# Ordering a weight load behind a one-column activation, and moving two small matmul events to the edges of a projection stage

## The chip, the cores and the metric

The kernel runs on one core of a Trainium2 chip. The metric is device time of one execution in microseconds (us), lower is better. Everything below is a matter of less than 1% of the time, so each comparison uses several runs, and the kernel before was timed again, on the same chip, beside every group of experiments (the four groups of experiments ran on four different chips). All runs reported here count as of the fast state, at a granted TensorE clock of 0.999 to 1.0, but for two runs of e9 at 0.996.

The engines are called TensorE (PE in the profile; PEld is its weight load), VectorE (DVE), ScalarE (ACT), GpSimd (POOL) and SyncE (SP). ACTq and SPq are the queues on which ScalarE and SyncE issue DMA transfers. PSUM is where the program puts TensorE's outputs; it does so in eight buffers of up to 512 columns, called banks here, four in the pool `ps_pj` and four in `ps_1`. A transfer has landed when the last of its completion marks has arrived, of which the packed traces show 16 for each transfer of the start; landing times here are read from these marks. The pitch is the time from one matmul's start to the next one's. Stages are called by the tile that TensorE writes in them: pk_ps (first projection), g_ps, kv_ps (KV), p_ps (projections of the V stage), q_ps (the quads).

## The reference, cut to what matters

Two attention blocks on the same x (2048 x 1024) are mixed by a sigmoid gate. Block A is linear attention, block B a dilated sliding window of 8 keys; 32 heads of 32.

```python
def phi(t): return where(t > 0, t + 1, exp(t)) + 1e-6
# A: pq, pk = phi(q), phi(k)
kv  = einsum("bhsd,bhse->bhde", pk, v)
num = einsum("bhqd,bhde->bhqe", pq, kv)
den = einsum("bhqd,bhd->bhq", pq, z)[..., None] + 1e-6   # z: pk summed over s
a   = (num / den) @ wo_A
# B: softmax over 8 earlier keys at distance 2, then @ wo_B      [cut]
out = g * a + (1 - g) * b
```

The kernel folds KV into A's output weight: the product of KV and `wo_A`, called W2 here, replaces `WoA` in place.

## The kernel before

The parts that the change touches, in the order in which TensorE meets them. At the start, the first projection (`pk`) needs `xT`, which comes by DMA transposes on SyncE's queue, and `WkA`, of which the first two quarters (k rows 0 and 1; column halves 0 and 1) come on ScalarE's queue. `project` runs the first k slice of half 0 for token tiles 0 to 3, of 128 tokens each (8 matmuls), then of half 1.

```python
load_wk(nc.scalar, 0, 0)                       # first quarter, 256 KB
first_act = consts.tile([P, 1], BF16, name="first_act")
nc.scalar.activation(out=first_act[:], in_=ones[:, 0:1], func=ACT.Exp)
load_wk(nc.scalar, 0, 1)                       # second quarter
load_xT(0, 0, 2)                               # transposes, SyncE
load_xT(0, 2, 4)
for k in range(1, 4):
    load_wk(nc.sync, k, 0); load_xT(k, 0, 4); load_wk(nc.sync, k, 1)
# ... [cut]
warm_up(37)                                    # 37 small matmuls
```

Later, KV is accumulated, then the V projection of B runs, with the four W2 events strewn into its first 64 matmuls, and with A's query projection (`qa`) from the fifth token tile on:

```python
for g in range(2):
    kvp = ps_1.tile([P, 4, 64], F32, name="kv_ps", tag="p1")
    # ... 64 matmuls of KV                       [cut]
    nc.vector.tensor_copy(out=KVT[:, 4 * g:4 * g + 4, :], in_=kvp[:])

def w2_event(g, half):
    def go():
        w2p = [ps_1.tile([P, 512], F32, name="w2_ps", tag="p1") for _ in range(4)]
        # ... 16 matmuls in 32x32 tiles of the array    [cut]
        for r in range(4):
            (nc.scalar.copy if r % 2 else nc.vector.tensor_copy)(
                out=WoA[half][:, 4 * g + r, :], in_=w2p[r][:])
    return go

def qa_finish(t, half, pj):
    phi(work, pq[:, half * 512:(half + 1) * 512], pj)
    if half == 1:
        normalize(t, pq, pn, prods[t % 2])      # about 4.7 us of VectorE
        nc.sync.dma_start(out=pqd[t * P:(t + 1) * P, :], in_=pn)

units = [u for t in range(4) for u in v_units(t)]
interleave(units, [(8 + 12 * (2 * g + half), w2_event(g, half)) for g in range(2) for half in range(2)])
for t in range(12):
    # ... v_units(4 + t), then qa_units(t)        [cut]
```

After that the four banks of `ps_1` are handed to the next stage: two to the scores and two to `po`, which VectorE fills with ones once. The next stage, the q_ps quads, accumulates four outputs in the four projection banks (`ps_pj`), slot by slot; the second quad can start its second slot only when the queries of the first quad have been copied out, partly by VectorE.

```python
po = ps_o.tile([P, 2, 512], F32, name="po")
nc.vector.memset(po[:], 1.0)
# evacuation of the queries of a quad
nc.scalar.activation(out=qz[:, 0, par, :], in_=ps[:], func=ACT.Copy, scale=qsel[:, 0:1])
nc.vector.tensor_scalar(out=qz[:, 1, par, :], in0=ps[:], scalar1=qsel[:, 1:2], scalar2=None, op0=ALU.mult)
```

VectorE's order is the program's in these stages; the fill of `po` alone stands outside.

The softmax here doesn't subtract the row's maximum and nothing guards it: scores larger than these inputs give would overflow.

## Time and profile before

| | before |
|---|---|
| median of the three first runs | 474.03 us |
| median of those and three more, beside the change | 473.86 us (473.54 to 475.84) |
| profiled run | 474.01 us, span 472.3 us |
| first weight matmul | 5.56 us |
| first KV matmul | 116.57 us |
| first q_ps matmul | 217.40 us |
| restart of the second quad's second slot | 226.37 us |

From the page of the kernel before, the busy time of each engine, and the shares of the chain of work that ended last:

```profile
PE 466.0 (99%) x5734; PEld 244.7 (52%) x5765; DVE 277.4 (59%) x601; ACT 169.1 (36%) x273; POOL 15.4 (3%) x30
...
PE 98%; DMA 1%; issue 0%; ACT 0%
```

TensorE has work for 99% of the span and is 98% of the chain. Whatever other engines do is free as long as TensorE doesn't wait for it, so the change can win only in the small gaps. The timeline of the first 9 us (columns: start, duration, engine, line, operation, output and input, count, and in brackets the idle time before it and what ended that):

```profile
0.80 2.60 SPq L94 DMA_TRANSPOSE xT<-in_A_x_dram  x2
...
0.83 0.96 ACTq L98 DMA_DIRECT2D WkA<-in_A_wqkv_dram  x2
...
2.09 0.20 ACT L106 ACTIVATE first_act<-const-bfloat16-1.0 128x1 bf16<-128x1 bf16 x1
...
5.55 0.13 PEld L169 LDWEIGHTS <-xT 128*128 128x128 bf16 x2 [0.88 <-DMA xT<-in_A_x_dram]
5.56 3.81 PE L169 MATMUL pk_ps<-WkA,xT 128*128 128x512 bf16 x14 [0.61 <-DMA xT<-in_A_x_dram]
```

Both weight quarters are issued before 1.8 us, the two transposes from 0.80 to 3.40. TensorE's weight load and matmul wait for the first transpose until 5.55. The stretches of 1 us in the same time (columns: stretch, length, then busy time and count of each engine, clock, share of the 16 DMA engines that is busy, GB/s):

```profile
4.00:5.00 1.00, 0.94 (x9) 0.67 (x7) 0.00 (x0) 0.00 (x0) 0.00 (x0) 1.00 1.17 289
5.00:6.00 1.00, 0.44 (x2) 0.17 (x3) 0.00 (x0) 0.00 (x0) 0.00 (x0) 1.00 0.95 233
6.00:7.00 1.00, 1.00 (x5) 0.42 (x4) 0.00 (x0) 0.00 (x0) 0.00 (x0) 1.00 1.25 284
```

From 4 to 7 us the busy share of the DMA engines is 0.95 to 1.25, as good as full (a share above 1 means that recorded packets overlap in time). TensorE's timeline in the kernel before, from KV into the V stage:

```profile
116.57 2.21 PE L240 MATMUL kv_ps<-G,WvA 128*64 128x64 bf16 x128
118.72 1.90 PE L295 MATMUL p_ps<-WvB,xT 128*128 128x512 bf16 x7
120.55 0.43 PE L283 MATMUL w_ps<-WoA,KVT 32*32 32x512 bf16 x16
120.91 2.76 PE L295 MATMUL p_ps<-WvB,xT 128*128 128x512 bf16 x12
123.61 0.43 PE L283 MATMUL w_ps<-WoA,KVT 32*32 32x512 bf16 x16
```

An event (w_ps) is followed by 12 V matmuls, and the next comes 3.06 us later, though 12 matmuls at their pitch of 0.216 us are 2.59 us: an event costs 0.47 us. Now VectorE's timeline at 131.9 us, with the fill of `po`:

```profile
131.89 0.91 DVE L372 MEMSET po<- 128x1024 f32 x1 [0.36 <-ACT tmp L300]
```

The fill ran in the middle of the V stage, where VectorE had little else to do (from 130.3 to 138.0 us it was busy for 2.15 us, the fill among them). Last, the timeline of the kernel before from 222 us, where the quads have begun:

```profile
222.71 1.29 DVE L321 TENSOR_TENSOR tmp<-tmp,den 128x512 bf16<-128x512 bf16 x2
...
224.85 1.41 DVE L427 TENSOR_SCALAR qz<-q_ps,qsel 128x512 bf16<-128x512 f32 x2 [0.85 <-PE q_ps L388]
225.63 0.69 ACT L425 ACTIVATE qz<-q_ps,qsel 128x512 bf16<-128x512 f32 x1 [0.20 <-DVE qz L427]
...
226.37 0.84 PE L388 MATMUL q_ps<-xT,WqB 64*64 64x512 bf16 x12
```

VectorE finishes the last normalize at 224.0 us, waits 0.85 us, and copies the queries; ScalarE's second copy waits for VectorE's first, and TensorE's slot starts when ScalarE is done, at 226.37.

### The profile page before, as it was taken

Reading aid. Unit: us, or ns where it says so; the run is one execution under the profiler, and the core shown is the slowest. Engines: PE = TensorE matmul, PEld = TensorE weight load, DVE = VectorE, ACT = ScalarE, POOL = GpSimd, SP = SyncE. Lnnn points to the kernel's source line nnn. Section 1 sums busy time; section 2 is a strip of 40 time slices with the busy share of each in tenths; the row PEclk is TensorE's granted clock in tenths of the full one; section 3 lists DMA queues with packets and bytes.
Section 4 is the critical chain, followed back from the end, with each engine's and each line's share of the span. In section 5 each row is a group of like instructions: output and inputs, shape, how many; then the busy total and the mean of one; then the engine's idle time right before and its main releaser. Section 6 shows DMA issues by size and latency. Waiting matters only on the chain.

```text
span 472.3 us, 13144 instructions
## 1 busy us (share of the span) xinstructions
PE 466.0 (99%) x5734; PEld 244.7 (52%) x5765; DVE 277.4 (59%) x601; ACT 169.1 (36%) x273; POOL 15.4 (3%) x30
## 2 busy tenths in 40 slices
PE   8999999999999999999999999999999999999997
PEld 5444444445444444445666666666664444444444
DVE  0496689990329999999567676767560049800000
ACT  1343321102443333333555555555551134221122
POOL 3300000500000000000000000000000000000000
PEclk9999999999999999999999999999999999999999
DMA  8999970000634233527326526452563933211001
GB/s 212 212 242 374 348 239 0 0 1 0 203 123 125 95 141 129 156 96 247 107 54 108 105 53 95 100 95 51 92 158 79 196 97 78 71 53 46 34 33 46
DMA packets 98780, 55.40 MB, mean 117 GB/s; under 512 B 70178, under 2 KB 90658, under 8 KB 98722
## 3 DMA queue, kind: packets, MB, share of 16 engines
q1 hardware_dynamic: 93282, 49.84, 41.1%
q10 hardware_dynamic: 5440, 4.72, 3.0%
q8 instruction: 45, 0.74, 0.7%
q14 instruction: 13, 0.11, 0.1%
HBM read 26.10 MB, written 15.86 MB: 89 GB/s over the span
## 4 chain that ended last, share of the span: by engine, by line
PE 98%; DMA 1%; issue 0%; ACT 0%
PE q_ps L388 27%; PE d_ps L585 12%; PE pk_ps L169 12%; PE p_ps L295 12%; PE g_ps L220 12%; PE e_ps L585 11%; PE p_ps L331 9%; PE po L467 2%; PE s2b L445 2%; DMA xT<-in_A_x_dram 1%; PE kv_ps L240 0%; PE w_ps L283 0%; ACT osb L590 0%
## 5 line engine op out<-in xcount | busy, mean ns | idle before, releaser
L388 PE MATMUL q_ps<-xT,WqB 64*64 64x512 bf16 x1024 | 68.3, 377 | 0.0
L388 PE MATMUL q_ps<-xT,WkB 64*64 64x512 bf16 x1024 | 67.9, 377 | 0.0
L156 DVE TENSOR_SCALAR e<-e 128x512 f32<-128x512 f32 x64 | 27.0, 423 | 64.3 <-ACT e L155 64.3
L295 PE MATMUL p_ps<-WvB,xT 128*128 128x512 bf16 x250 | 57.3, 379 | 0.5 <-issue 0.3
L169 PE MATMUL pk_ps<-WkA,xT 128*128 128x512 bf16 x251 | 55.6, 381 | 0.9 <-DMA xT<-in_A_x_dram 0.6
L220 PE MATMUL g_ps<-pk,xrow 128*128 128x512 bf16 x251 | 55.2, 379 | 0.3
L450 ACT ACTIVATE PT<-s2b 128x928 bf16<-128x928 f32 (+4 forms) x40 | 34.2, 854 | 45.5 <-PE s2b L445 45.5
L452 DVE TENSOR_TENSOR PT<-PT,mask 128x928 bf16<-128x928 bf16 (+4 forms) x40 | 23.6, 590 | 38.2 <-ACT PT L450 38.2
L331 PE MATMUL p_ps<-WqA,xT 128*128 128x512 bf16 x187 | 43.1, 379 | 0.3
L585 PEld LDWEIGHTS <-pqT 128*128 128x128 bf16 x272 | 26.0, 98 | 29.8 <-issue 0.4
L585 PEld LDWEIGHTS <-OBT 128*128 128x128 bf16 x272 | 26.0, 98 | 29.3
L169 PEld LDWEIGHTS <-xT 128*128 128x128 bf16 x256 | 25.1, 98 | 31.2 <-DMA xT<-in_A_x_dram 0.9
L220 PEld LDWEIGHTS <-xrow 128*128 128x128 bf16 x256 | 25.0, 98 | 30.2
L295 PEld LDWEIGHTS <-xT 128*128 128x128 bf16 x256 | 24.6, 98 | 30.0 <-issue 0.9
L388 PEld LDWEIGHTS <-WkB 64*64 64x64 bf16 x1024 | 31.7, 107 | 15.4 <-issue 0.4
L388 PEld LDWEIGHTS <-WqB 64*64 64x64 bf16 x1024 | 31.4, 106 | 15.4 <-issue 0.7
L155 ACT ACTIVATE e<-pk_ps 128x512 f32<-128x512 f32 x32 | 18.9, 597 | 40.8 <-PE pk_ps L169 36.6
L300 ACT CAST tmp<-p_ps 128x512 bf16<-128x512 f32 x32 | 18.8, 590 | 37.9 <-PE p_ps L295 29.2
L585 PE MATMUL d_ps<-WoA,pqT 128*128 128x512 bf16 (+1 forms) x133 | 30.7, 369 | 0.2
L585 PE MATMUL d_ps<-WoB,OBT 128*128 128x512 bf16 (+1 forms) x134 | 30.7, 369 | 0.1
L331 PEld LDWEIGHTS <-xT 128*128 128x128 bf16 x192 | 18.8, 98 | 22.7
L585 PE MATMUL e_ps<-WoB,OBT 128*128 128x512 bf16 (+2 forms) x133 | 29.7, 363 | 0.2
(62 smaller groups left out, 484.6 us busy)
## 6 DMA issues: line engine op xcount, KB each, us to landing
vd<-tmp SPq DMA_DIRECT2D x16, 264.0 KB
xrow<-in_A_x_dram SPq DMA_DIRECT2D x4, 1024.0 KB
out_dram<-osb ACTq DMA_DIRECT2D x31, 128.0 KB
pqd<-tmp SPq DMA_DIRECT2D x12, 256.0 KB
WvA<-in_A_wqkv_dram SPq DMA_DIRECT2D x2, 1024.0 KB
WoA<-in_A_wo_dram SPq DMA_DIRECT2D x2, 1024.0 KB
WvB<-in_B_wqkv_dram SPq DMA_DIRECT2D x2, 1024.0 KB
WqA<-in_A_wqkv_dram SPq DMA_DIRECT2D x2, 1024.0 KB
```

What stands on the lines that cost most here:

```text
L155: nc.scalar.activation(out=e[:], in_=pj[:], func=ACT.Exp)
L156: nc.vector.tensor_scalar(out=e[:], in0=e[:], scalar1=1.0, scalar2=1e-6, op0=ALU.min, op1=ALU.add)
L169: nc.tensor.matmul(pj[:], lhsT=xT[:, kt, t * P:(t + 1) * P], rhs=WkA[half][:, kt, :], start=(kt == 0), stop=(kt == KT - 1))
L220: nc.tensor.matmul(pj[:], lhsT=xrow[:, t, kt * P:(kt + 1) * P], rhs=pk[:, t, half * 512:(half + 1) * 512], start=(t == 0), stop=(t == NB - 1))
L295: nc.tensor.matmul(st["pj"][:], lhsT=xT[:, kt, t * P:(t + 1) * P], rhs=WvB[half][:, kt, :], start=(kt == 0), stop=(kt == KT - 1))
L300: nc.scalar.copy(out=v[:, half * 16:(half + 1) * 16, 0:Dh], in_=st["pj"][:].rearrange("p (h e) -> p h e", h=16))
L331: nc.tensor.matmul(st["pj"][:], lhsT=xT[:, kt, t * P:(t + 1) * P], rhs=WqA[half][:, kt, :], start=(kt == 0), stop=(kt == KT - 1))
L388: nc.tensor.matmul(banks[o][64 * j:64 * j + 64, :], lhsT=lhsT(r, kt, j), rhs=rhs(r, kt), start=first and kt == 0, stop=kt == KT - 1, skip_ ...
L445: nc.tensor.matmul(s2b[64 * par:64 * par + 64, pair, :, o:o + w], lhsT=kts[c][r, par, k0:k0 + 64], rhs=qz[r, :, par, q0 % 512:q0 % 512 + w ...
L450: nc.scalar.activation(out=pt[:, :, 0:W_], in_=s2b[:].rearrange("p a b s -> p (a b) s")[:, :, 0:W_], func=ACT.Exp, scale=SCALE)
L452: nc.vector.tensor_tensor(out=pt[:, :, 0:W_], in0=pt[:, :, 0:W_], in1=mask[:, None, base:base + W_].broadcast_to([P, 4, W_]), op=ALU.mult)
L585: nc.tensor.matmul(st["ps"][:, 0:n], lhsT=lhsT, rhs=W[c0 // 512][:, c, c0 % 512:c0 % 512 + n], start=(side == 0 and c == 0), stop=(side == ...
```

## The change

Its intent has three parts. The one-column activation writes into the tile of the second weight quarter, so that quarter must wait for it, and the transposes get the DMA engines first. KV is accumulated in the projection banks, so that the first W2 event can stand directly behind KV. The first and the last W2 event move to the two edges of the V stage, where TensorE changes its tiling anyway (in the profile from `128*64` in KV to `128*128` in the V stage, and from there to `64*64` in the quads).

```diff
         load_wk(nc.scalar, 0, 0)
-        first_act = consts.tile([P, 1], BF16, name="first_act")
-        nc.scalar.activation(out=first_act[:], in_=ones[:, 0:1], func=ACT.Exp)
+        nc.scalar.activation(out=WkA[1][:, 0, 0:1], in_=ones[:, 0:1], func=ACT.Exp)
         load_wk(nc.scalar, 0, 1)
 ...
-                kvp = ps_1.tile([P, 4, 64], F32, name="kv_ps", tag="p1")
+                kvp = ps_pj.tile([P, 512], F32, name="kv_ps", tag="pj")[:, 0:256].rearrange("p (c d) -> p c d", c=4)
 ...
-                nc.vector.tensor_copy(out=KVT[:, 4 * g:4 * g + 4, :], in_=kvp[:])
+                nc.vector.tensor_copy(out=KVT[:, 4 * g:4 * g + 4, :], in_=kvp)
 ...
-            interleave(units, [(8 + 12 * (2 * g + half), w2_event(g, half)) for g in range(2) for half in range(2)])
+            w2_event(0, 0)()
+            interleave(units, [(20, w2_event(0, 1)), (32, w2_event(1, 0))])
             for t in range(12):
 ...
+            w2_event(1, 1)()
             WqB = load_w("WqB", B_wqkv, 0, "wc")
```

## The prediction

> What bounds it. TensorE is busy 466.0 of 472.3 us in the page's engine table, and the chain of waits is 98% TensorE, at granted clock 1.0. Time is won only where TensorE waits or switches, so I expect a change below 1 us.
>
> Start. The waits of the first 12 us put TensorE's first real matmul, at 5.56 us, down to the first xT transpose (last landing 5.52). The first WkA quarter had landed by 3.89, the second by 5.20. DMA packets come in blocks: first quarter to 3.1 us, first transpose to about 3.9, second quarter 3.6 to 4.4, and only at 4.4 the transpose's 4-byte completion writes and the second transpose. [...] After the change the second quarter waits for the one-column activation (2.09 to 2.30, after the table load), so it issues at about 2.35 instead of 1.35. The first quarter's packets came 1.09 us after issue: estimate 3.45, barely before the 3.6 at which they flow now. If the completion write slips ahead, the first matmul starts up to 0.8 us earlier; otherwise nothing happens. I expect 0.4. Later loads have at least 1.4 us of slack, so the gain would stay. The second quarter is needed 1.7 us after the first matmul: no new wait.
>
> V stage edges. An inner W2 event costs 0.47 us (period of 12 V matmuls plus event 3.06, less 12 x 0.216): 0.37 of its own and 0.1 of switching. [...] At the edges the events share a switch that is paid anyway (KV to V costs 0.22 extra, projection to the q_ps quads 0.09). Gain about 0.25 us. KV in the projection banks lets the first event start without waiting for KV's second copy (ends 119.26); the first copy ends 118.24, before KV's matmuls at 118.7.
>
> The cost. The last event's copies now fall on VectorE behind the last normalize, which ends at 224.0. Two of them take 1.29, and the fill of po (0.91), done at 131.9 so far, needs banks that those copies free, so it will probably follow them. The queries' VectorE copies start at 224.85 now, and the next quad's second slot already waits for them (226.38 instead of 226.08). VectorE after the change, by my estimate: 223.5 + 1.29 + 0.91 = 225.7, so that slot starts 0.9 us later. If the fill comes after the queries' copies the loss is about zero. I weigh this at 0.6. Score banks are free by 225, before 227.
>
> Sum: -0.4 - 0.25 + 0.6, about zero. I predict 473.8 us, range 473.0 to 474.8; chances 0.01 faster by over 2%, 0.98 within, 0.01 slower.
>
> To check. The second WkA load issues near 2.35 us; the first transpose lands before 5.0 (gain) or at 5.5 (none); the stretch from the last g_ps matmul to the first q_ps matmul shrinks by 0.1 to 0.3 us; the po fill sits near 225 us on VectorE, and TensorE waits about 1 us at the second quad.
>
> Wrong if: a later transpose lands later, so that TensorE starves in the first 10 us; or the fill delays the scores as well (over 1 us); or the fill is placed where VectorE is idle, so that only gains remain (near 473.2).

Two sentences are cut from it, as marked: they told of the hardware in general. The sum came to -0.4 - 0.25 + 0.6 = -0.05 us. That the DMA packets came in blocks is read from the trace of the kernel before; what orders the blocks was not shown, so that the completion might slip ahead is the author's estimate. Of the 0.47 us of an event the 0.1 of switching is read from the pitch of 0.31 instead of 0.216 us ahead of each event.

## The result, and the profile after

| | before | after |
|---|---|---|
| median of six runs | 473.86 us (473.54 to 475.84) | 475.69 us (474.84 to 477.11) |
| profiled run | 474.01 us, span 472.3 us | 475.38 us, span 473.7 us |
| first weight matmul | 5.56 us | 4.74 us |
| first KV matmul | 116.57 us | 117.03 us |
| first q_ps matmul | 217.40 us | 217.64 us |
| restart of the second quad's second slot | 226.37 us | 227.71 us |

The ratio of the times is 1.0039, with a 95% interval of 1.0014 to 1.0063. Ratios here and below are the mean time of one kernel's fast runs over that of the other's fast runs of the same rounds, so not quite the ratio of the medians quoted. The change is slower by about 0.4%, and since the interval lies above 1 that is not noise. The measured median lies above the predicted range of 473.0 to 474.8.

The rows of the table, subtracted stage by stage, locate the difference of the two profiled runs. Up to KV the change loses 0.46 us, although its first matmul is 0.82 us earlier. From KV to the quads it takes 100.61 instead of 100.83 us, a gain of 0.22. From the first q_ps matmul to the restart it takes 10.07 instead of 8.97 us, a loss of 1.10. The rest of the span is the same within 0.1 us.

The same two lines of the page, for the change:

```profile
PE 468.0 (99%) x5765; PEld 244.7 (52%) x5765; DVE 277.2 (59%) x601; ACT 169.2 (36%) x273; POOL 15.3 (3%) x30
...
PE 80%; DVE 17%; DMA 1%; issue 1%; ACT 1%; SPq 0%; DVEq 0%; ACTq 0%
```

TensorE's busy time hardly differs, but the chain is now 17% VectorE. That is not 17% of the time lost: the last thing that TensorE waited for, ScalarE's query copy at 227 us, had itself waited for VectorE's copy at 226 us, and behind that the chain follows VectorE's own queue back through the stage of the normalizes, which VectorE fills nearly as tightly as TensorE does (from 170 to 217 us VectorE is busy for 45.0 of the 47.0 us, TensorE for all 47.0). It shows where the wait is, not how long it is. The timeline of the change's first 9 us (the transposes are issued as before):

```profile
0.82 0.45 ACTq L98 DMA_DIRECT2D WkA<-in_A_wqkv_dram  x1
...
2.09 0.20 ACT L105 ACTIVATE WkA<-const-bfloat16-1.0 128x1 bf16<-128x1 bf16 x1
2.32 0.40 ACTq L98 DMA_DIRECT2D WkA<-in_A_wqkv_dram  x1
...
4.74 1.91 PE L168 MATMUL pk_ps<-WkA,xT 128*128 128x512 bf16 x4
...
7.28 1.90 PE L168 MATMUL pk_ps<-WkA,xT 128*128 128x512 bf16 x8 [0.63 <-DMA xT<-in_A_x_dram]
```

The second quarter is issued at 2.32 us, as intended, and the first weight matmul starts at 4.74. But after four matmuls TensorE waits until 7.28 us, for xT: it needs the second transpose, which landed at 5.91 us in the kernel before and lands at 7.23 here. The change's stretches of 1 us:

```profile
4.00:5.00 1.00, 1.00 (x10) 0.89 (x9) 0.00 (x0) 0.00 (x0) 0.00 (x0) 1.00 0.63 125
5.00:6.00 1.00, 1.00 (x3) 0.30 (x2) 0.00 (x0) 0.00 (x0) 0.00 (x0) 1.00 1.08 256
6.00:7.00 1.00, 0.65 (x2) 0.00 (x0) 0.00 (x0) 0.00 (x0) 0.00 (x0) 1.00 1.11 275
```

From 4 to 5 us the DMA engines move 125 GB/s at a busy share of 0.63, where they moved 289 at 1.17. On average they are idle for over a third of that microsecond, so it isn't simply their bandwidth that runs short. The packets of the second transpose and of the second quarter run mixed from about 4.0 to 6.2 us, both slowly; in the kernel before the quarter's packets ran from 4.0 to 4.4 us and none of a transpose did. The matmul counts tell one more thing: three matmuls from 5 to 6 us, where TensorE doesn't wait. They stand 0.427 us apart instead of 0.216. TensorE runs at half rate here, as it does for two matmuls in the profile of the kernel before. TensorE's timeline in the change, from KV into the V stage:

```profile
117.03 2.22 PE L239 MATMUL kv_ps<-G,WvA 128*64 128x64 bf16 x128
119.17 0.43 PE L282 MATMUL w_ps<-WoA,KVT 32*32 32x512 bf16 x16
119.54 4.49 PE L294 MATMUL p_ps<-WvB,xT 128*128 128x512 bf16 x20
123.96 0.43 PE L282 MATMUL w_ps<-WoA,KVT 32*32 32x512 bf16 x16
```

The first event follows KV with no wait for a copy or a bank, and the 20 V matmuls behind it run unbroken. From KV to the 33rd V matmul, with three events in either kernel, it takes 10.36 instead of 10.46 us. And the timeline of the change from 217 us:

```profile
217.28 0.43 PE L282 MATMUL w_ps<-WoA,KVT 32*32 32x512 bf16 x16
...
222.59 1.29 DVE L320 TENSOR_TENSOR tmp<-tmp,den 128x512 bf16<-128x512 bf16 x2
...
223.81 1.28 DVE L286 CAST WoA<-w_ps 128x512 bf16<-128x512 f32 x2
...
225.44 0.91 DVE L373 MEMSET po<- 128x1024 f32 x1 [0.36 <-DVE WoA L286]
...
226.26 1.32 DVE L428 TENSOR_SCALAR qz<-q_ps,qsel 128x512 bf16<-128x512 f32 x2
226.97 0.69 ACT L426 ACTIVATE qz<-q_ps,qsel 128x512 bf16<-128x512 f32 x1 [1.50 <-DVE qz L428]
...
227.71 0.84 PE L389 MATMUL q_ps<-xT,WqB 64*64 64x512 bf16 x12 [1.24 <-ACT qz L426]
```

The last normalize ends at 223.9 us, 0.1 us earlier than before. Then come the event's two copies (WoA, 1.28 us), 0.36 us in which VectorE is idle, and the fill of `po` (0.91 us), which now needs banks that these copies free, and only then the queries. ScalarE's second query copy waits 1.50 us for VectorE, and TensorE's slot starts at 227.71, after a wait that the profile gives as 1.24 us.

### The profile page after: what moved, and what is told of

The parts are those of the page before. It is cut to its first block, busy times and chain, and to the rows that moved or that the text cites. A ratio compares the mean times of both kernels' runs of the same rounds, so it can differ in the third digit from the quotient of the medians.

```text
span 473.7 us, 13175 instructions
## 1 busy us (share of the span) xinstructions
PE 468.0 (99%) x5765; PEld 244.7 (52%) x5765; DVE 277.2 (59%) x601; ACT 169.2 (36%) x273; POOL 15.3 (3%) x30
## 3 DMA queue, kind: packets, MB, share of 16 engines
q10 hardware_dynamic: 5440, 4.72, 3.1%
## 4 chain that ended last, share of the span: by engine, by line
PE 80%; DVE 17%; DMA 1%; issue 1%; ACT 1%; SPq 0%; DVEq 0%; ACTq 0%
PE q_ps L389 25%; PE d_ps L586 12%; PE g_ps L219 12%; PE pk_ps L168 12%; PE e_ps L586 11%; PE p_ps L294 4%; DVE tmp L156 3%; DVE tmp L311 3%; DVE den L313 3%; DVE tmp L320 3%; PE po L468 2%; DVE e L155 2%; PE s2b L446 2%; DMA xT<-in_A_x_dram 1%; DVE den L316 1%; PE p_ps L330 1%
## 5 line engine op out<-in xcount | busy, mean ns | idle before, releaser
L586 PE MATMUL e_ps<-WoA,pqT 128*128 128x512 bf16 (+2 forms) x136 | 30.0, 364 | 0.0
```

Of the source, the lines that this page charges most:

```text
L586: nc.tensor.matmul(st["ps"][:, 0:n], lhsT=lhsT, rhs=W[c0 // 512][:, c, c0 % 512:c0 % 512 + n], start=(side == 0 and c == 0), stop=(side == ...
```

## The experiments

All kernels gave correct results. In every group the kernel before ran beside them; its median was 473.86, 473.56, 473.67 and 473.76 us in the four groups. Each experiment is described by its edit against the kernel before, unless it says otherwise.

### Taking the change apart: e1 to e4

e1 is the change with its first part undone (the activation writes `first_act` again). e2 is the kernel before with only that first part. e3 has the KV banks and the first edge; e4 has the last edge alone.

```diff
 e3
-                kvp = ps_1.tile(...)                    # KV in ps_pj, as in the change
+            w2_event(0, 0)()
+            interleave(units, [(20, w2_event(0, 1)), (32, w2_event(1, 0)), (44, w2_event(1, 1))])
 e4
+            interleave(units, [(8, w2_event(0, 0)), (20, w2_event(0, 1)), (32, w2_event(1, 0))])
 ...
+            w2_event(1, 1)()
             WqB = load_w("WqB", B_wqkv, 0, "wc")
```

> The change with its first part taken back: the one-column activation again writes a tile of its own, so the second weight quarter issues at about 1.35 us. Theory (two losses and one gain: start +0.45 us because the second xT transpose lands 1.3 us late, edges -0.22, late po fill and copies on VectorE +1.1): first weight matmul back at 5.56 us, TensorE without a pause of 1.3 us before 7.3 us, second quad slot still about 1.1 us late, time about 0.9 us over the kernel before and less spread than the change. Rival (the held-back quarter is harmless or a gain, as the prediction had it): time as the change or higher, 1.8 us or more over the kernel before.

> The kernel before with only the held-back second quarter. Theory: first weight matmul near 4.75 us, then a wait of over 1 us for the second transpose, the g_ps stage starts 0.4 to 0.5 us later than before, time +0.45 us (up to +1 in runs where the DMA blocks interleave worse; runs spread by over 1 us). Rival (prediction): -0.4 us.

> The kernel before with KV in the projection banks and only the first W2 event moved to the edge; the last stays at unit 44. Theory: gains about 0.1 to 0.15 us (a shared switch) and costs nothing: fill of po still near 131 us. Rival (moving KV to the projection banks makes the V matmuls wait for banks): 0 or slower by over 0.1 us, with a wait ahead of the first p_ps matmuls.

> The kernel before with only the last W2 event moved behind the last projection. Theory: the event's two VectorE copies and the po fill fall between the last normalize and the queries' copies; the second quad slot starts near 227.3 instead of 226.38 us; time +0.9 to +1.0 us net of about 0.1 us gained. Rival (the loss of the change is all in the start): time the same or 0.1 us less.

| kernel | median (range), us | against before, 473.86 | ratio, 95% interval |
|---|---|---|---|
| e1, both edges, old start | 474.42 (474.32 to 474.53) | +0.56 | 1.0009, 0.9996 to 1.0023 |
| e2, new start alone | 475.03 (474.44 to 476.30) | +1.17 | 1.0023, 1.0005 to 1.0042 |
| e3, KV banks and first edge | 473.69 (473.48 to 475.81) | -0.17 | 1.0001, 0.9983 to 1.0020 |
| e4, last edge alone | 474.68 (474.49 to 476.81) | +0.82 | 1.0028, 1.0007 to 1.0049 |

By the medians the three parts add up: 1.17 - 0.17 + 0.82 = 1.82 us, and the change itself measured 475.69 - 473.86 = 1.83. That the two agree so closely is luck: each interval reaches 0.8 to 0.9 us to either side, and the ratios of the means add up to 0.52%, where the change has 0.39% (two of e4's six runs lie 2 us above its others). What holds is that the start and the last edge lose about 1 us each. Which of them loses more isn't settled: the medians put the start first, the ratios the last edge. The small gain of the first edge is inside the noise as timed. e1 and e3 alone would not be distinguishable from the kernel before; e2 and e4 are slower. e1 was expected at +0.9 us and came out at +0.56.

e2's start is worse than I expected (+0.45). In its profile the first transpose lands only at 6.01 us and the second at 8.03. The view of TensorE's weight-load waits in e2's first 12 us (engine and line, what it waited for: us in total, times, longest):

```profile
PEld L168 <- DMA xT<-in_A_x_dram: 3.2, 2, 1.7
```

So the change doesn't even bring the first transpose forward reliably. Its last landing was 4.57 us in the first profile of the change, 6.01 in e2, and 5.31 in a second profile of the change (e11 below), against 5.22 to 5.59 in the six kernels that keep the old start and warm-up (the kernel before, e1, e3, e4, e5, e6). The second transpose landed at 7.23, 8.03 and 7.59 us with the hold, against 5.42 to 5.91 in those six.

The difference of the two first profiles, 0.46 us, was also a small sample of the loss: the profiled run of the kernel before, 474.01 us, was one of its slower ones, with two matmuls at half rate. In e1 and e4, which start like it, the g_ps stage begins at 60.7 and 60.9 us, in the profiled run before at 61.2, and with the held-back quarter at 61.7, 62.0 and 62.5 us.

### What delays the quads: e5 and e6

Both are built on e1, so without the new start. e5 puts the fill behind the queries' copies in VectorE's order; e6 leaves the fill to be placed as before and moves the last event's VectorE copies to ScalarE.

```diff
 e5
-            nc.vector.memset(po[:], 1.0)
 ...
+            events.append((36, lambda: nc.vector.memset(po[:], 1.0)))
 e6
-                        (nc.scalar.copy if r % 2 else nc.vector.tensor_copy)(
+                        (nc.scalar.copy if r % 2 or (g, half) == (1, 1) else nc.vector.tensor_copy)(
```

> The change with the start undone (474.42 us), and the po fill placed in VectorE's order after the queries' copies of the first quad. Theory: the fill's 0.91 us leaves the chain, the two W2 copies stay in it; from the first q_ps matmul to the restart of the second quad's second slot 9.1 to 9.3 us (10.06 with the fill ahead, 8.98 in the kernel before); time 473.5 us. Rival (not the fill but another thing in the move of the last event, as its banks or the extra TensorE work, costs the time): slot as late as before the edit, time 474.4.

> The change with the start undone, and all four copies of the last W2 event on ScalarE, which is idle there. The compiled order then has the fill inside the last normalize, ahead of all queries' copies, and no W2 copy on VectorE. Theory: VectorE is done with the fill and the normalize at about the same 224.3 to 224.9 us as the queries need, slot 8.9 to 9.1 us after the first q_ps matmul, time 473.5 us or a little less. Rival as in e5: 474.4.

e5 took 473.20 us (473.03 to 473.26), ratio 0.9990 (0.9977 to 1.0003); e6 took 473.48 us (473.23 to 473.54), ratio 0.9996 (0.9983 to 1.0008); the kernel before 473.56 (473.46 to 474.13, nine runs). The timeline of e5 from 216 us:

```profile
216.69 1.92 PE L389 MATMUL q_ps<-xT,WkB 64*64 64x512 bf16 x32
...
222.86 1.28 DVE L287 CAST WoA<-w_ps 128x512 bf16<-128x512 f32 x2
...
224.06 1.40 DVE L428 TENSOR_SCALAR qz<-q_ps,qsel 128x512 bf16<-128x512 f32 x2
224.83 0.69 ACT L426 ACTIVATE qz<-q_ps,qsel 128x512 bf16<-128x512 f32 x1 [0.31 <-DVE qz L428]
...
225.57 0.84 PE L389 MATMUL q_ps<-xT,WqB 64*64 64x512 bf16 x12
...
225.67 0.91 DVE L507 MEMSET po<- 128x1024 f32 x1 [0.21 <-DVE qz L428]
```

From the first q_ps matmul to the restart it takes 8.88 us in e5 and 8.77 in e6, against 10.06 in e1. Moving the fill alone takes away 1.18 us of the stage, more than the fill's own 0.91 because the idle 0.36 us ahead of it goes too, and 1.22 us of the time (474.42 to 473.20, though from groups on different chips; counted from the kernel before of each group, +0.56 to -0.36, it is 0.92). The rival, that the moved event costs something by its banks or its TensorE work, falls. The event's two copies alone cost next to nothing there: VectorE is done with them at 224.06 us, and ScalarE could start on the first queries at 223.84, so at most 0.2 us is lost. In e6 the fill went into a gap in the normalize, and nothing is lost either.

e5 is the best version. All its five runs are below all nine of the kernel before in the same rounds, by 0.36 us at the median, but the interval of the ratio still touches 1, so this is a gain of about 0.1% at the median, and not a secured one.

### Where the second quarter belongs: e7, e9, e14, e13

e7 takes the second quarter off ScalarE's queue and issues it on SyncE's, behind the second transpose. e9 and e14 keep it on ScalarE's queue and hold it longer, by larger activations into it.

```diff
 e7
-        load_wk(nc.scalar, 0, 1)
         load_xT(0, 0, 2)
         load_xT(0, 2, 4)
+        load_wk(nc.sync, 0, 1)
 e9     two activations of 128x1024 into WkA[1] instead of first_act
 e14    two activations of 128x512 into WkA[1] instead of first_act
```

> The kernel before, with the second weight quarter issued on the SyncE queue behind the second transpose instead of on the ScalarE queue. If the loss of the held-back quarter comes from its packets interleaving with the second transpose (theory), both transposes now land early: first matmul near 4.75 us, no wait at the fifth matmul, second quarter landing near 6.5 us, time -0.3 to -0.8 us against before. Rival (any later second quarter starves TensorE): a new wait of half a microsecond or more at the ninth matmul or at the next loads, time the same or longer.

> The kernel before, with the second quarter held back on the ScalarE queue as in the change, but by two activations of 128x1024 into it: issue at about 4.2 us by estimate instead of 2.33. Theory (the loss of the change is the second quarter's packets alternating with the second transpose's): the second transpose lands at about 5.3 us as in e7, although the queue is ScalarE's; the second quarter lands near 7 us and TensorE waits for it at the ninth matmul; time near e7, 473.5 to 474.2 us, and shorter than with the hold to 2.33 (475.0). Rival (the ScalarE queue itself, or any hold, delays the transpose): second transpose again at 7 us or later, time 475 or more.

> The kernel before, the second quarter held back on the ScalarE queue by two activations of 128x512, issue at about 3.4 us by estimate, as the second transpose's issue ends (3.40). Both theories A and B: the second transpose lands before 5.8 us, the second quarter near 6.5 to 7 us; no wait at the fifth matmul, a short one at the ninth; time 473.3 to 474. If the transpose still lands at 7 us or later, the overlap with the issue of the transpose isn't what matters (A by bytes still in flight).

| kernel | second quarter issued | second transpose landed | second quarter's last landing | median, us |
|---|---|---|---|---|
| before | 1.35 | 5.91 | 5.20 | 473.56 to 473.86 |
| the change | 2.33 | 7.23 (7.59 in e11) | 7.02 (7.36) | 475.69, with the edges |
| e2, its start alone | 2.33 | 8.03 | 7.80 | 475.03 (474.44 to 476.30) |
| e14 | 3.41 | 5.68 | 8.02 | 474.12 (473.63 to 474.43) |
| e7 | 3.44 | 5.30 | 7.03 | 473.72 (473.60 to 473.99) |
| e9 | 4.74 | 5.28 | 9.20 | 477.26 (475.56 to 478.60) |

In these profiles, one of each kernel, only the whole quarter that is issued while the second transpose is being issued (2.16 to 3.40 us) delays it past 7 us. Earlier or later it doesn't, and the queue doesn't matter: e9 holds it on ScalarE's queue and the transpose lands as in e7. But holding longer moves the wait from the transpose to the quarter itself. In e9 and e14 TensorE waits at the ninth matmul, which needs half 1. The line for it in the waits of e9's first 12 us (engine and line, what it waited for: us in total, times, longest):

```profile
PE pk_ps L169 <- DMA WkA<-in_A_wqkv_dram: 2.2, 1, 2.2
```

And in those of e14:

```profile
PE pk_ps L169 <- DMA WkA<-in_A_wqkv_dram: 1.3, 1, 1.3
```

My expectation for e9, near e7, was wrong: each activation took 1.06 us, the issue came at 4.74 instead of 4.2, behind loads that SyncE had put in meanwhile, and the quarter landed 2.2 us after e7's. Two of e9's four runs (478.17 and 478.60 us) were granted a clock of 0.996, so its median is too high to compare; the two at 0.999 and 1.0 took 475.56 and 476.34, still above every run of the kernel before in their group (474.07 at most). e14 missed its expectation too: the transpose landed early as expected, but the quarter at 8.02 instead of 6.5 to 7 us, the wait at the ninth matmul was 1.3 us and not short, and the median is just above the 473.3 to 474 expected. e7 has no such wait, yet gains nothing: 473.72 against 473.56 us, ratio 1.0002 (0.9990 to 1.0015). In its profile TensorE starts at 4.76 us but runs its first four weight matmuls at half rate, and in e8 below, where the rate is full sooner, it waits 0.4 us for the second quarter instead. The expected -0.3 to -0.8 us was a miss. In each profile of the table with the quarter held back, the transpose or the quarter landed at 7.0 us or later.

The last question was how a copy issued inside the transpose's issue delays it: by its bytes (theory A), or by being issued there, whatever its bytes (theory B; a guess in the recorded text at how that would come about is cut, as no run shows it). e13 issues 8 KB of the quarter (16 columns) at the hold and the other 496 columns behind the transpose.

```diff
-        first_act = consts.tile([P, 1], BF16, name="first_act")
-        nc.scalar.activation(out=first_act[:], in_=ones[:, 0:1], func=ACT.Exp)
-        load_wk(nc.scalar, 0, 1)
+        nc.scalar.activation(out=WkA[1][:, 0, 0:1], in_=ones[:, 0:1], func=ACT.Exp)
+        nc.scalar.dma_start(out=WkA[1][:, 0:2, 0:16], in_=...)      # 256 descriptors of 32 bytes
         load_xT(0, 0, 2)
         load_xT(0, 2, 4)
+        nc.sync.dma_start(out=WkA[1][:, 0:2, 16:512], in_=...)
```

> Only 8 KB of the second quarter (16 of its 512 columns, 256 descriptors of 32 bytes) is issued on the ScalarE queue behind the one-column activation, at about 2.33 us, inside the issue of the second transpose (2.16 to 3.40); the other 496 columns go to the SyncE queue behind that transpose, as in e7. Theory A (the bytes of the quarter share the DMA engines with the transpose's packets): the second transpose lands at 5.2 to 5.8 us, as in e7 (5.30), time within 0.4 us of e7's 473.72. Theory B [...]: it lands at 6.5 us or later and TensorE waits over 0.5 us at the fifth matmul.

The second transpose landed at 6.08 us: later than in e7 (5.30), earlier than in the change (7.23 and 7.59), and between what the two theories demand. The whole quarter (7.23, 7.59 and 8.03 us) delays it by 1.9 to 2.7 us against e7, the 8 KB by 0.8, with the same number of descriptors by the program's shapes (256; the trace of the kernel before shows the whole quarter as 256 packets of 1 KB). So the larger part of the delay goes with the amount of data. It isn't simply lack of bandwidth: in the change the busy share from 4 to 5 us was only 0.63. That the issue alone carries the rest is a weak sign: this is one profile, and 6.08 is only 0.2 us beyond the latest landing of a kernel with no copy in that place (5.91). The time, 474.24 us (473.74 to 475.05), ratio 1.0001 (0.9976 to 1.0027), doesn't tell, since this profile also has a pause at 351 us that belongs to something else (see e10). How the DMA hardware divides the work between the two stays open.

### Both mended, and runs that stand apart: e8, e10, e11, e12

e8 is e6 and e7 together. e10 is the kernel before with `warm_up(46)`, e12 is e5 with it, e11 is the change once more.

> e6 and e7 together: both edges with the last copies on ScalarE, and the second quarter behind the second transpose. If the parts add: 0.2 to 0.3 us under before from the edges and 0.3 to 0.8 from the start, 473.0 us or less; this would beat both kernels by a little. If the start still has two states, some runs lie 2 us higher.

> The kernel before with 46 instead of 37 warm-up matmuls, so that TensorE is busy nearly until the first transpose lands. Theory of the runs 2 us above the rest (e3's profile, a run of 475.81, shows ten matmuls at a pitch of 0.427 us instead of two): [...] Without the pause no run should lie over 475 us, and the median stays within 0.3 us of before. Rival (the high runs are something else): high runs still occur, now and then.

> The change itself once more, for its spread and a second look at the start: median 475.0 to 476, some runs near 477; the second transpose lands at 7 us or later and TensorE waits over 1 us at the fifth matmul. If it lands before 6 us in this profile, the start theory is in doubt.

> e5 (both edges, fill after the queries' copies, start as before) with the longer warm-up of e10. Expected 473.0 to 473.3 us with no high run; the best version of the study if e10 does no harm.

e8: 473.27 us (472.88 to 473.55), ratio 0.9991 (0.9978 to 1.0005): above the 473.0 expected, as good as e5 and no better, so e7's start adds nothing that these runs could show. e11: 475.56 us (474.90 to 477.03), ratio 1.0042 (1.0031 to 1.0054), which confirms the result in another group, with the second transpose at 7.59 us as said; the wait at the fifth matmul was 0.85 us beyond the pitch, not over 1.

Some runs of some kernels lie 2 us above the rest (475.84 of the kernel before; 476.81 and 476.66 of e4), and others more than 1 us (477.01 and 477.11 of the change). e3's profile fell into one, at 475.81 us. Its stretches of 1 us, TensorE alone (busy time and count, clock, DMA):

```profile
6.00:7.00 1.00, 1.00 (x4) 1.00 1.19 240
7.00:8.00 1.00, 1.00 (x4) 1.00 0.99 208
8.00:9.00 1.00, 1.00 (x3) 1.00 0.93 261
...
10.00:11.00 1.00, 1.00 (x6) 1.00 0.61 120
```

Four matmuls or fewer in a microsecond until 10 us, where the kernel before has five or six: eleven pitches of 0.35 to 0.43 us before 0.216 is reached, so about 2 us are lost. The clock column says 1.00 all the same, because the trace holds no clock record of those first microseconds. The time at which the pitch changed differed from trace to trace: before the first weight matmul in e4, after two in the kernel before, after ten in e3. The packed traces' own clock records agree: full clock is recorded from 3.81 us in e4, 6.41 in the kernel before and 10.13 in e3. This explains e3's run. What sets that time was not shown, and that the other high runs have the same cause is likely from their size, but they were not profiled.

e10 was to test the guess that TensorE's pause before the first weight matmul (0.61 us in the kernel before) decides when the pitch changes, and failed to. It took 474.81 us (474.07 to 475.22), ratio 1.0021 (1.0008 to 1.0034), a full 1.1 us slower, where within 0.3 was expected, and two runs lie over 475 (475.15 and 475.22). No run is 2 us above the rest, but five runs are too few to tell. The loss isn't at the start (q_ps begins at 217.0 us, before the 217.4 of the kernel before). It is here, in TensorE's timeline at 351 us:

```profile
350.86 0.61 PE L388 MATMUL q_ps<-WqA,xT 64*64 64x512 bf16 x5
352.60 1.71 PE L388 MATMUL q_ps<-WqA,xT 64*64 64x512 bf16 x28 [1.14 <-ACT raw L549]
```

TensorE stands still from about 351.1 to 352.6 us. The wait that the profile names (ACT raw, done at 352.4) explains most of it only at first sight: in the kernel before the same copies end at 352.7, and TensorE's 36 matmuls at 351.19 don't wait for them. What does differ is the queue that the page calls "q8 instruction": the packed trace shows 45 packets of 16 KB on it in the kernel before, in this stage mostly every 3.5 to 5.6 us, but in e10 one, the 39th, starts at 350.2, 6.7 us after its predecessor, among the `WoB` loads that SyncE issues from 348 us on. The same packet tells the kernels apart in all 16 profiles. In thirteen it starts 4.2 to 5.0 us after its predecessor, and there is no pause at 351 us. In the other three the pause grows with the delay: 5.9 us in e12, 6.3 in e13 and 6.7 in e10, with pauses of 0.6, 0.9 and 1.3 us over the pitch. That the late packet causes the pause was not tested, and why it comes late is not known. e12 took 474.02 us (473.87 to 474.69), ratio 1.0009 (0.9997 to 1.0021), with that pause of 0.6 us, where 473.0 to 473.3 was expected, and is no improvement on e5.

## Why the prediction was wrong

- What bounds the kernel: right. TensorE is the chain, and nothing of the change shows in busy time.
- The start: wrong, and this is the step that failed. The prediction said "Later loads have at least 1.4 us of slack, so the gain would stay", and expected 0.4 us of gain. The second transpose was left out of that count. It landed at 5.91 us in the kernel before and the first weight load that reads it ran at 6.62 (its matmul at 6.83), so it had 0.7 us, and less than none once the first matmul moves forward by 0.8. Held back by 1 us, the second quarter left the company of the first transpose and joined that of the second, which then landed at 7.23 to 8.03 us. Measured alone (e2) the start costs 1.17 us at the median instead of gaining 0.4. How the transfers delay one another there stays open. The prediction named this outcome under "Wrong if", but gave it no weight in the sum. Its other half, that the first transpose's completion may slip ahead, was seen once (4.57 us) and not in the two other profiles with that hold (5.31 and 6.01); with the quarter issued after 3.4 us it was seen in all four profiles (4.64 to 4.72 in e7, e8, e9 and e14).
- The edges: right in kind. 0.25 us was expected; the profiles show 0.22 from KV to the quads, and e5, with both edges and nothing else of consequence, is 0.36 us under the kernel before. The explanation by shared switches fits the 0.31 instead of 0.216 us that stand ahead of each event in the kernel before; what TensorE does in that time was not measured by itself.
- The KV banks: right. The first event follows KV directly, and the profile names no wait ahead of it.
- The fill: right, mechanism and place (near 225 us, behind the two copies; restart about 0.9 us late predicted). It was under-weighed: 0.6 us went into the sum, for the chance that the fill might fall elsewhere, and e5, with the fill moved, shows that it cost 0.9 to 1.2.
- The sum: -0.4 - 0.25 + 0.6 against measured +1.17 - 0.17 + 0.82, of which the last two hold edges and fill together. With the start at +1.17 and the rest as predicted it would have been about 475.4, counted from 473.86.

## What to carry to other kernels

When a transfer is held back, list every transfer that will be in flight at its new time, and the slack of each against its first consumer, not only of those that come later; here the one issued at the same moment had the least. When work moves to the edge of a stage, look at what else is tied to its buffers: a fill that was free in the middle of the stage became, with the idle time ahead of it, 1.2 us of critical path at its end, and one line that orders it behind the urgent copies gave that back. Where TensorE is the bound from first to last, expect tenths of a microsecond from such moves (the best here, e5, gained 0.36 us at the median), and don't trust one profile for a start that differs from one to the next: the first transpose landed at 4.57 and 5.31 us in two profiles of the change, and full clock was recorded from 3.81, 6.41 and 10.13 us in three kernels that start alike.
